# Score matmuls of the 90-row chunks over 40 columns, loads tied to the mixing, and one group's first layer on row halves of the array

## The chip, the core and the metric

One core of a Trainium2 chip runs the kernel. TensorE shows in the profile as PE (matmuls) and PEld (weight loads), VectorE as DVE, ScalarE as ACT, GpSimd as POOL, SyncE as SP; SP, POOL and, at the start, ACT also issue DMA transfers. The metric is the device time of one execution in microseconds (us), median of several runs.

## The reference

Talking-heads attention, then a two-layer network with a leaky activation. Shapes: batch 4, 12 heads, 448 tokens, head width 64; the network goes 768 -> 2048 -> 768.

```python
scores = scale * np.matmul(q, k.transpose(0, 1, 3, 2))
scores = np.einsum('bhij,hg->bgij', scores, w_pre)
scores = scores - np.max(scores, axis=-1, keepdims=True)
attn = np.exp(scores)
attn = attn / (np.sum(attn, axis=-1, keepdims=True) + 1e-09)
attn = np.einsum('bhij,hg->bgij', attn, w_post)
attn_out = np.matmul(attn, v)          # -> x, 1792 x 768
h = x @ w_in
g = np.maximum(h, 0.0) + alpha * np.minimum(h, 0.0)
out = g @ w_out
```

## The kernel before

**First phase (attention).** The 448 query rows of a batch are cut into four chunks of 120, 120, 120 and 90 rows (the last overlaps its neighbour by two). That gives 16 chunks, `ci` 0 to 15; chunks 3, 7, 11 and 15 have 90 rows. The steps, with the letter that the planner uses:

- **Q** (`qk`, L286): a score unit, one pair of heads of one chunk, six units in a chunk. It is four matmuls: two head halves (rows 0 to 63 and 64 to 127 of the array) by two column blocks of the chunk's query rows. The second block is what is left after 64: 56 columns for a 120-row chunk and 26 for a 90-row chunk. Each such float32 matmul stands in the trace as two instructions, so a unit is x8.
- **S** (`qk_out`, L299): ACT or DVE copies a unit's scores to SBUF.
- **L** (`relay`, L306): a DMA carries ten query rows of all heads into the layout that the mixing needs (tiles `sr`, eight buffers), issued by SP and POOL in turn.
- **M** (`mix`, L313): two relayed groups times the pre-mixing weights. There are 90. **R** (L318, DVE) takes the row maximum, **E** (L325, ACT) the exponentials, **N** (L331 to L335, DVE) the normalised post-mixing weights, **P** (`post`, L347, PE) the post-mixing, and **A** (L359, ACT or DVE) copies its result out.
- **V** (`pv`, L369): attention times values, two for each chunk; **XH**, **XL** (L383, L385) round the result into a high and a low part and **W** (L391) stores them.
- Loads: **LQ** (L263) the queries of a chunk, **LK** (L254) a pair of key tiles, **LV** (L270, L271) the values of a batch, **F** (L397) a 768 KB block of 64-bit weights, which **C** (L57 to L63, seven DVE operations) turns into float32. All four are issued on POOL's queue, where relays stand too.

Every engine works through its instructions in program order. The function `plan` writes that order once, at build time: a list scheduler with a cost for each step, a priority, predecessors and buffer counts. `at` is the earliest planned time of a step. A predecessor in the plan only orders the steps; an instruction itself waits for data and buffers alone.

**Second phase (network).** `FGROUPS` cuts the 16 blocks of hidden units into five groups; a unit `u` is one block `f` for one batch `bl`, 64 units in all, in the order group, batch, block. A unit's first layer `l1` (L541) is 18 matmuls of 128 rows x 128 columns over 448 tokens into one PSUM tile `h` (the pool has two buffers), then `act_op`: j=0 a scaled Relu on ACT (L554), j=1 on DVE (L556), j=2 and j=3 split the result into `g` (L558, L560). The second layer `l2` (L579) is 18 matmuls into six accumulators. PE's order is l1(u), l2(u-1), l1(u+1), l2(u), and so on. Group 4 (blocks 12 to 15) takes the batches in the order 0, 1, 2, 3, so units 52 to 55 are its batch 1.

Of the kernel before, what the change touches and what calls it, by code (L numbers as in the profile page):

```python
# [8 lines left out]
F32 = mybir.dt.float32  # L9
# [5 lines left out]
ALU = mybir.AluOpType  # L15
# [4 lines left out]
B, H, S, D = 4, 12, 448, 64  # L20
# [9 lines left out]
NCC = DM // 128  # L30
NFC = DFF // 128
NP = H // 2
# [3 lines left out]
RAHEAD = 3  # L36
# [2 lines left out]
FGROUPS = [[0, 1, 2], [3, 4, 5], [6, 7, 8], [9, 10, 11], [12, 13, 14, 15]]  # L39
NPRE = 3  # L40
NXS = 3
COST = {"Q": 0.82, "M": 0.82, "P": 1.0, "V": 2.15, "U": 3.7, "mode": 0.15, "R": 1.09, "E": 1.37, "N": 0.68}
HOP, DRAIN = 0.07, 0.2
LOOK = 0.3
# [21 lines left out]
def plan(groups, first, chunk_list):  # L66
# [5 lines left out]
    def op(name, engs, prio, preds=(), acq=(), rel=(), at=0.0):  # L72
        if isinstance(engs, tuple):
            engs = [engs]
        ops[name] = (engs, prio, list(dict.fromkeys(preds)), acq, rel, at)

    pe = lambda kind, mode="q": ("PE", COST[kind], DRAIN, mode)
    act = lambda d: ("ACT", d, HOP, "")
    dve = lambda d: ("DVE", d, HOP, "")
    dma = lambda d, l=3.0: ("DMA", d, l, "")  # L80

    for ci, (b, c) in enumerate(chunk_list):
        op(("LQ", ci), dma(1.0) if ci >= 2 else dma(0.0, 0.0), first[max(ci - 1, 0)] / 2 - RAHEAD - 5, acq=(("q", ci),))
        for p in range(NP):
            n = ci * NP + p
            prio = (n - NP) * 0.92 - 1
            op(("Q", ci, p), pe("Q"), prio, [("LQ", ci), ("LK", b, p // 2)], (("slot", (ci, p)),) + ((("st", ci),) if p == 0 else ()),
               ((("q", ci),) if p == NP - 1 else ()) + ((("k", b, p // 2),) if c == len(CHUNKS) - 1 and p % 2 else ()),
               at=5.5 + 1.1 * p if ci == 0 else 10.0)
            op(("S", ci, p), [act(0.92), dve(1.09)], prio, [("Q", ci, p)], rel=(("slot", (ci, p)),))  # L90
    for b in range(B):
        f4 = first[4 * b]
        for kk in range(NP // 2):
            op(("LK", b, kk), dma(1.2) if b else dma(0.0, 0.0), f4 / 2 - RAHEAD - 11 + kk, acq=(("k", b, kk),))
        op(("LV", b), dma(3.0), f4 / 2 + (4 if b else 0), acq=(("v", b),), at=18.0)
    for n, (ci, r) in enumerate(groups):
        op(("L", n), dma(0.8, 4.0), n / 2 - 1 - RAHEAD, [("S", ci, p) for p in range(NP)], (("sr", n),),
           (("st", ci),) if n + 1 == first[ci + 1] else ())
# [1 line left out]
    for m in range(NB):  # L100
# [5 lines left out]
        for g in range(2):  # L106
            ci = groups[2 * m + g][0]
            op(("A", m, g), [act(0.52), dve(0.63)], m + 1.7, [("P", m)],
               (("at", ci),) if 2 * m + g == first[ci] else (), (("pa", m),))
    for ci, (b, c) in enumerate(chunk_list):  # L110
        lb = (first[ci + 1] - 1) // 2
        mine = [("A",) + divmod(n, 2) for n in range(first[ci], first[ci + 1])]
        for hx in range(2):
            pr = lb + 3.3 + 1.5 * hx
# [5 lines left out]
    nh = 2 * NPRE  # L120
    for i in range(nh):
        pr = 6 + 11 * i
        op(("F", i), dma(2.0, 4.0), pr - 6, acq=(("cr", i),), at=20.0)
        for j in range(7):
            op(("C", i, j), dve((0.57, 0.57, 0.57, 0.96, 0.57, 0.96, 0.96)[j]), pr + 1.3 * j,
               [("C", i, j - 1) if j else ("F", i)] + ([("C", i - 1, 6)] if i and not j else []),
               (("ct", i),) if j == 1 else (), (("cr", i),) if j == 5 else ())
        op(("WS", i), dma(1.0), pr + 10, [("C", i, 6)], rel=(("ct", i),))
# [3 lines left out]
    for f in range(NPRE):  # L132
        op(("LW", f), dma(2.0, 6.0), NB - 9 + f, [("WS", i) for i in range(nh)], (("cr", ("w", f)),))
        for x in range(2):
            pr = NB - 3 + 1.2 * f + 0.6 * x
# [3 lines left out]
    for u in range(2):  # L139
# [6 lines left out]

    cap = {"slot": 3, "st": NXS, "sr": 2 * (RAHEAD + 1), "e": LAG + 1, "r": LAG + 1, "pa": 1, "at": 2, "q": 3, "k": 4, "v": 1,
           "xe": 2, "cr": 2, "ct": 2}
# [14 lines left out]
    while ready:  # L163
        best = None
        for n in ready:
            engs, prio, preds, acq, rel, at = ops[n]
# [3 lines left out]
            for e, d, l, md in engs:  # L170
                d += COST["mode"] if e == "PE" and md != mode else 0.0
                t = max(t0, idle[e])
# [26 lines left out]
def talking_heads_prelu(ctx: ExitStack, tc: tile.TileContext, q, k, v, w_pre, w_post, mask, w_in, w_out, alpha, out):  # L199
    nc = tc.nc  # L200
# [5 lines left out]
    groups, first = [], []  # L206
# [29 lines left out]
    ps = pool("ps", 1, p1, space=PSUM)  # L236
# [10 lines left out]
    k_t, q_t, v_t, s_t, a_t = {}, {}, {}, {}, {}  # L247
# [9 lines left out]
    def load_q(ci, dmas=None):  # L257
        b, c = chunk_list[ci]
        c0, cn = CHUNKS[c]
        q_t[ci] = qp.tile([128, NP * CW], F32, tag="q", name=f"q{ci}")  # L260
        for hf in range(2):
            dma = dmas[hf] if dmas else nc.gpsimd
            dma.dma_start(out=q_t[ci][64 * hf:64 * hf + 64, :NP * cn],  # L263
                          in_=q[b, :, QOFF[c] + NP * hf * cn:QOFF[c] + NP * (hf + 1) * cn])
# [10 lines left out]
    def slot_tile(i, name):  # L275
        return ps.tile([128, 2, 512], F32, tag=f"b{i}", name=name)

    def qk(ci, p, slot):
        b, c = chunk_list[ci]
        cn = CHUNKS[c][1]  # L280
        ps = slot_tile(slot, f"s{ci}_{p}")
        for hf in range(2):
            for ch in range(2):
                r = slice(64 * hf, 64 * hf + 64)
                i0, i1 = 64 * ch, min(64 * ch + 64, cn)
                nc.tensor.matmul(ps[i0:i1, hf, :S], q_t[ci][r, p * cn + i0:p * cn + i1], k_t[b, p // 2][r, p % 2, :],  # L286
                                 start=True, stop=True)
        u_t["qk", ci, p] = ps
# [132 lines left out]
    with tc.manual_schedule():  # L421
        start = p1r.enter_context(tc.tile_pool(name="start", bufs=1, side="right"))
# [24 lines left out]
        for i, w in enumerate((w_pre, w_post)):  # L447
# [15 lines left out]
            op=ALU.mult,  # L463
        )
        P2 = {}
# [8 lines left out]
        x_t, wi_t, wo_t, g_t, h_t, accs = {}, {}, {}, {}, {}, {}  # L474
# [59 lines left out]
        def l1(u, slot=None):  # L534
            gi, bl, f = units[u]
            w, x = wi_t[f], x_t[bl].bitcast(F32R)
            ps = P2["h"].tile([128, 512], F32, tag="h", name=f"h{u}") if slot is None else slot_tile(slot, f"h{u}")[:, 0]
            i = 0
            for cc in range(NCC):
                for tw, tx in ((0, 0), (0, 1), (1, 0)):  # L540
                    nc.tensor.matmul(ps[:, :S], w[:, tw, cc * 128:(cc + 1) * 128], x[:, tx, cc, :],  # L541
                                     start=(i == 0), stop=(i == 3 * NCC - 1))
                    i += 1
            h_t[u] = ps

        def act_op(u, j):
            f = units[u][2]
            h = h_t[u][:, :S]
            if j == 0:
                g_t[u] = (P2["gp"].tile([128, S], F32, tag="t", name=f"t{u}"),  # L550
                          P2["gp"].tile([128, 2, S], F32R, tag="g", name=f"g{u}"))
            t, g = g_t[u]
            if j == 0:
                nc.scalar.activation(out=t, in_=h, func=AF.Relu, scale=-1.0)  # L554
            elif j == 1:
                nc.vector.scalar_tensor_tensor(out=t, in0=t, scalar=oma[:, f:f + 1], in1=h, op0=ALU.mult, op1=ALU.add)  # L556
            elif j == 2:
                nc.scalar.copy(g[:, 0], t)  # L558
            else:
                nc.vector.tensor_tensor(g[:, 1], t, g[:, 0], ALU.subtract)  # L560
# [105 lines left out]
        def prefetch(u):  # L666
            nxt = []
            for _, bl, _ in units[u:]:
                if bl not in nxt:
                    nxt.append(bl)  # L670
                if len(nxt) == NXS:
                    break
            for bl in nxt[1:]:
                if bl not in x_in.values():
                    free = [i for i in range(NXS) if x_in.get(i) not in nxt]
                    load_x(bl, free[0])
# [54 lines left out]
```

## Time and profile before

| | us |
|---|---|
| median of 3 runs | 931.24 (928.26 to 932.08) |
| profiled execution, device time | 935.73 |
| its span, first to last instruction | 934.0 |
| PE busy in the span | 878.8 (94%) |
| DVE busy | 578.4 (62%) |
| ACT busy | 343.5 (37%) |

Busy shares are means over two phases that differ. The prediction therefore reads stretches: how busy each engine is between two moments, what PE waited for just before a matmul, and how far apart the starts of two neighbouring groups on PE lie. The printed duration of a matmul reaches past the start of the next one, since matmuls are pipelined; the distance of starts is what a group costs.

### The profile page before, as it was taken

The page shows a single profiled execution, that of the slowest core. Times are in us where ns is not written, and L with a number is a line of the kernel's source. Part 1 is how long each engine was busy: PE and PEld are TensorE (multiplying, and loading weights), DVE is VectorE, ACT ScalarE, POOL GpSimd, SP SyncE. Part 2 cuts the span into 40 slices and gives each one's busy share as a digit, 9 for nine tenths or more (in the row PEclk, how much of TensorE's full clock was granted, in tenths as well). Part 3 has the DMA queues.
Part 4 walks back from the last instruction along what each step waited for, and adds up shares of the span by engine and source line. Part 5 has one row for each costly group of instructions (what it writes and reads, how often), then busy time and mean ns, then how long its engine had stood idle before and what let it go on. Part 6 is the DMA issues. An engine that isn't in the chain of part 4 may idle for free.

```text
span 934.0 us, 23852 instructions
## 1 busy us (share of the span) xinstructions
PE 878.8 (94%) x10380; PEld 665.5 (71%) x10380; DVE 578.4 (62%) x1023; ACT 343.5 (37%) x718; POOL 110.6 (12%) x194
## 2 busy tenths in 40 slices
PE   8589998999889997998899999999999999979998
PEld 3354565456553665456899999999999999869997
DVE  4475787569854886456455566667666763873332
ACT  3453765357643675346222222121212211211110
POOL 5122223222311222000000000000000000000000
PEclk9799999999999999999999999999999999989999
DMA  7666677566754469754831242025012511232111
GB/s 194 188 191 154 185 220 205 157 197 181 217 156 129 137 204 251 225 175 131 259 151 34 68 151 70 34 68 185 35 34 68 186 34 35 68 106 106 60 60 59
DMA packets 70974, 125.36 MB, mean 134 GB/s; under 512 B 32614, under 2 KB 59246, under 8 KB 70870
## 3 DMA queue, kind: packets, MB, share of 16 engines
q0 software_dynamic: 15344, 59.22, 21.8%
q1 hardware_dynamic: 54866, 63.33, 21.4%
q8 instruction: 81, 1.33, 0.6%
q10 hardware_dynamic: 660, 1.30, 0.5%
q14 instruction: 23, 0.19, 0.1%
HBM read 66.16 MB, written 18.92 MB: 91 GB/s over the span
## 4 chain that ended last, share of the span: by engine, by line
PE 82%; DVE 6%; DMA 6%; ACT 3%; issue 2%; SPq 0%; POOL 0%; ACTq 0%; DVEq 0%; POOLq 0%
PE h L541 25%; PE acc L579 24%; PE s L286 13%; PE x L369 8%; PE pa L347 7%; PE m L313 7%; DMA sr<-st 5%; DVE at L359 1%; DVE nm L318 1%; ACT e L325 1%; DVE ao L591 1%; ACT st L299 1%; ACT at L359 1%; DMA k<-in_k_dram 1%; DVE ct L60 0%
## 5 line engine op out<-in xcount | busy, mean ns | idle before, releaser
L541 PE MATMUL h<-x,w 128*128 128x448 f32 x1152 | 250.5, 370 | 6.4 <-ACT w L504 6.3
L579 PE MATMUL acc<-g,w 128*128 128x448 f32 x1152 | 245.6, 366 | 2.0 <-DVE t L556 1.4
L541 PEld LDWEIGHTS h<-x,w 128*128 128x128 f32 x1152 | 217.3, 189 | 28.8 <-ACT w L504 6.7
L579 PEld LDWEIGHTS acc<-g,w 128*128 128x128 f32 x1152 | 216.1, 188 | 21.7 <-DVE t L556 1.7
L286 PE MATMUL s<-k,q 64*64 64x448 f32 (+2 forms) x768 | 159.9, 555 | 1.9 <-ACT st L299 0.6
L347 PEld LDWEIGHTS pa<-r,e 64*64 64x64 f32 x5040 | 100.0, 136 | 58.7 <-issue 33.2
L556 DVE SCALAR_TENSOR_TENSOR t<-t,oma,h 128x448 f32<-128x448 f32 x64 | 43.5, 680 | 157.8 <-ACT t L554 157.8
L554 ACT ACTIVATE t<-h 128x448 f32<-128x448 f32 x64 | 34.9, 545 | 268.1 <-PE h L541 268.1
L325 ACT ACTIVATE e<-m,nm 128x448 f32<-128x448 f32 x180 | 112.7, 636 | 31.6 <-DVE nm L318 20.4
L318 DVE TENSOR_REDUCE nm<-m 128x2 f32<-128x896 f32 x90 | 97.6, 1085 | 36.1 <-PE m L313 35.7
L347 PE MATMUL pa<-r,e 64*64 64x60 f32 x5040 | 105.8, 223 | 14.6 <-issue 9.4
L313 PE MATMUL m<-sr,wk 64*64 64x448 f32 x720 | 97.7, 566 | 21.6 <-DMA sr<-st 18.4
L286 PEld LDWEIGHTS s<-k,q 64*64 64x64 f32 (+2 forms) x768 | 37.2, 128 | 78.2 <-issue 65.0
L369 PEld LDWEIGHTS x<-at,v 128*64 128x64 f32 x1536 | 75.6, 138 | 20.1 <-issue 6.6
L359 DVE COPY at<-pa 128x480 f32<-128x480 f32 x83 | 53.8, 656 | 54.8 <-ACT at L359 30.4
L306 POOL DMA_DIRECT2D sr<-st x89 | 53.2, 600 | 286.2 <-PE m L313 189.6
L369 PE MATMUL x<-at,v 128*64 128x120 f32 (+1 forms) x1536 | 82.5, 264 | 3.7 <-DVE at L359 1.4
L299 ACT COPY st<-s 120x896 f32<-120x896 f32 (+1 forms) x65 | 58.6, 906 | 67.7 <-PE s L286 61.2
L359 ACT COPY at<-pa 128x480 f32<-128x480 f32 x97 | 53.8, 570 | 69.7 <-PE pa L347 55.1
L313 PEld LDWEIGHTS m<-sr,wk 64*64 64x64 f32 (+1 forms) x720 | 24.9, 134 | 55.1 <-DMA sr<-st 22.2
L558 ACT CAST g<-t 128x448 fp32r<-128x448 f32 x64 | 36.3, 567 | 53.9 <-DVE t L556 53.9
L591 DVE TENSOR_TENSOR ao<-ao,acc 128x448 f32<-128x448 f32 x96 | 52.7, 613 | 1.7 <-PE acc L579 1.7
(49 smaller groups left out, 522.3 us busy)
## 6 DMA issues: line engine op xcount, KB each, us to landing
x<-x SPq DMA_DIRECT2D x16, 1344.0 KB
sr<-st SPq DMA_DIRECT2D x89, 210.0 KB
sr<-st POOLq DMA_DIRECT2D x89, 210.0 KB, 4.8
cr<-in_w_in_dram POOLq DMA_DIRECT2D x16, 768.0 KB, 4.7
cr<-in_w_out_dram POOLq DMA_DIRECT2D x16, 768.0 KB, 4.6
x<-xe SPq DMA_DIRECT2D x48, 180.0 KB
out_dram<-ao SPq DMA_DIRECT2D x24, 224.0 KB
v<-in_v_dram POOLq DMA_DIRECT2D x4, 1152.0 KB, 9.3
```

The costliest lines, as they stand in the source:

```text
L286: nc.tensor.matmul(ps[i0:i1, hf, :S], q_t[ci][r, p * cn + i0:p * cn + i1], k_t[b, p // 2][r, p % 2, :], start=True, stop=True)
L299: copy(dst[:cn, p], u_t.pop(("qk", ci, p))[:cn, :, :S])
L306: dma.dma_start(out=sr_t[n][SR0:SR0 + GP], in_=s_t[ci][r:CHUNKS[chunk_list[ci][1]][1]:CHUNKS[chunk_list[ci][1]][1] // GI])
L313: nc.tensor.matmul(ps[hf:hf + 64, u, :S], wk[r, :], g[r, :], start=True, stop=True)
L318: nc.vector.tensor_reduce(out=nm, in_=m_t[m][:, :, :S], axis=AX.X, op=ALU.max, negate=True)
L325: nc.scalar.activation(out=e_t[m][:, u], in_=m_t[m][:, u, :S], func=AF.Exp, bias=nm_t[m][:, u:u + 1], scale=1.0, accum_out=se_t[m][:, u:u ...
L347: nc.tensor.matmul(dst[:, :, HI * u:HI * u + HI], e[h, u, 64 * jb:64 * jb + 64], r[h, u].rearrange("p (h i) -> p h i", h=H), start=True, s ...
L359: copy_on[eng](dst, pa[:, g, :NS * GP].rearrange("p (s i) -> p s i", i=GI))
L369: nc.tensor.matmul(ps[64 * t:64 * t + 64, 0, cl * CW:cl * CW + cn], v_t[b][:, s, h * D:(h + 1) * D], a_t[ci][:, s, h, :cn], start=(s == 0) ...
L541: nc.tensor.matmul(ps[:, :S], w[:, tw, cc * 128:(cc + 1) * 128], x[:, tx, cc, :], start=(i == 0), stop=(i == 3 * NCC - 1))
L579: nc.tensor.matmul(accs[c][:, :S], w[:, tw, c * 128:(c + 1) * 128], g[:, tg], start=(f == fs[0] and i == 0), stop=(f == fs[-1] and i == 2))
L591: nc.vector.tensor_tensor(acc_sb[c, bl], acc_sb[c, bl], accs[c][:, :S], ALU.add)
```

## The change

Three edits. (1) In `qk` the second column block of a 90-row chunk is 40 columns wide instead of 26; the extra columns read the next head's queries, or, for the last head, 14 zeroed columns that a POOL memset writes. Their output rows are not read. (2) In `plan`, the loads LQ, LK, LV and F get a mixing step M as predecessor, in place of a planned time for LV and F. (3) The first layer of units 52 to 55 runs as pairs of matmuls on rows 0 to 63 and 64 to 127 into two PSUM tiles, which ACT (a copy) and DVE (an addition) then bring together.

```diff
+MIN_M = 40
+ROWS = (4, 1)
...
-        op(("LQ", ci), dma(1.0) if ci >= 2 else dma(0.0, 0.0), first[max(ci - 1, 0)] / 2 - RAHEAD - 5, acq=(("q", ci),))
+        op(("LQ", ci), dma(1.0) if ci >= 2 else dma(0.0, 0.0), first[max(ci - 1, 0)] / 2 - RAHEAD - 5,
+           [("M", first[ci - 1] // 2 - RAHEAD - 7)] if ci > 3 else [("M", ci - 2)] if ci >= 2 else [], acq=(("q", ci),))
...
-            op(("LK", b, kk), dma(1.2) if b else dma(0.0, 0.0), f4 / 2 - RAHEAD - 11 + kk, acq=(("k", b, kk),))
-        op(("LV", b), dma(3.0), f4 / 2 + (4 if b else 0), acq=(("v", b),), at=18.0)
+            op(("LK", b, kk), dma(1.2) if b else dma(0.0, 0.0), f4 / 2 - RAHEAD - 11 + kk,
+               [("M", f4 // 2 - RAHEAD - 12 + kk)] if b else [], acq=(("k", b, kk),))
+        op(("LV", b), dma(3.0), f4 / 2 + (4 if b else 0), [("M", f4 // 2 + 2)], acq=(("v", b),))
...
-        op(("F", i), dma(2.0, 4.0), pr - 6, acq=(("cr", i),), at=20.0)
+        op(("F", i), dma(2.0, 4.0), pr - 6, [("M", pr - 3)], acq=(("cr", i),))
...
+        pad = 64 + MIN_M - cn
+        if pad > 0:
+            nc.gpsimd.memset(q_t[ci][:, NP * cn:NP * cn + pad], 0.0)
...
-                i0, i1 = 64 * ch, min(64 * ch + 64, cn)
+                i0, i1 = 64 * ch, 64 * ch + 64 if not ch else max(cn, 64 + MIN_M)
...
+            if (gi, bl) == ROWS:
+                ps2 = P2["h"].tile([128, 512], F32, tag="h", name=f"h{u}_2")
+                h_t[u, 2] = ps2
...
-                    nc.tensor.matmul(ps[:, :S], w[:, tw, cc * 128:(cc + 1) * 128], x[:, tx, cc, :],
-                                     start=(i == 0), stop=(i == 3 * NCC - 1))
+                    st = dict(start=(i == 0), stop=(i == 3 * NCC - 1))
+                    if (gi, bl) == ROWS:
+                        for r, o in ((0, ps), (64, ps2)):
+                            nc.tensor.matmul(o[:, :S], w[r:r + 64, tw, cc * 128:(cc + 1) * 128], x[r:r + 64, tx, cc, :], **st)
+                    else:
+                        nc.tensor.matmul(ps[:, :S], w[:, tw, cc * 128:(cc + 1) * 128], x[:, tx, cc, :], **st)
...
+            if (u, 2) in h_t:
+                if j == 0:
+                    hs_t[0] = P2["gp"].tile([128, S], F32, tag="hs", bufs=1, name=f"hs{u}")
+                hs = hs_t[0]
+                if j == 0:
+                    nc.scalar.copy(t, h_t[u, 2][:, :S])
+                    nc.vector.tensor_tensor(hs, t, h, ALU.add)
+                h = hs
```

On PE, a score unit of a 90-row chunk (chunk 3, first unit, and the P and M behind the second) stood so before:

```order
L286 MATMUL s_0_848<-k_0_122,q_463 64x448
L286 MATMUL s_0_848<-k_0_122,q_463 26x448
L286 MATMUL s_0_848<-k_0_122,q_463 64x448
L286 MATMUL s_0_848<-k_0_122,q_463 26x448
L286 MATMUL s_1_857<-k_0_122,q_463 64x448
```

and stands so now:

```order
L293 MATMUL s_0_848<-k_0_122,q_504 64x448
L293 MATMUL s_0_848<-k_0_122,q_504 40x448
L293 MATMUL s_0_848<-k_0_122,q_504 64x448
L293 MATMUL s_0_848<-k_0_122,q_504 40x448
L293 MATMUL s_1_858<-k_0_122,q_504 64x448
```

The place is the same and the number of matmuls too; only the width of every second one differs.

On POOL's queue, right after the constants have been loaded (q, k, v are loads, `cr` is F's block, `sr` are relays), the order before was:

```order
L263 DMA q_177<-in_q_dram 64x720 x2
L254 DMA k_0_180<-in_k_dram 64x896 x2
L306 DMA sr_111<-st_188 120x1x448
L306 DMA sr_108<-st_188 120x1x448
L306 DMA sr_106<-st_188 120x1x448
L269 MEMSET v_277 64x768
L270 DMA v_277<-in_v_dram 128x3x768
L271 DMA v_277<-in_v_dram 64x768
L397 DMA cr_0_308<-in_w_in_dram 128x768
L306 DMA sr_108<-st_188 120x1x448
```

and is now:

```order
L313 DMA sr_111<-st_182 120x1x448
L313 DMA sr_108<-st_182 120x1x448
L313 DMA sr_106<-st_182 120x1x448
L270 DMA q_264<-in_q_dram 64x720 x2
L313 DMA sr_112<-st_182 120x1x448
L313 DMA sr_109<-st_182 120x1x448
L276 MEMSET v_299 64x768
L277 DMA v_299<-in_v_dram 128x3x768
L278 DMA v_299<-in_v_dram 64x768
L404 DMA cr_0_357<-in_w_in_dram 128x768
```

The queries of chunk 2 moved behind three relays, the first key load of batch 1 left this stretch, and the values and the first weight block moved behind two more relays, whose buffers the first two mixings set free.

On ACT, the first two units of the batch on row halves (units 52 and 53) stood before as the Relu and the cast of each unit:

```order
L554 ACTIVATE t_9069<-h_9032 128x448
L558 CAST g_9070<-t_9069 128x448
L554 ACTIVATE t_9115<-h_9075 128x448
L558 CAST g_9116<-t_9115 128x448
L554 ACTIVATE t_9176<-h_9133 128x448
L558 CAST g_9177<-t_9176 128x448
```

and now, from the same unit 51 on, as:

```order
L578 ACTIVATE t_9073<-h_9036 128x448
L582 CAST g_9074<-t_9073 128x448
L574 COPY t_9138<-h_2_9080 128x448
L578 ACTIVATE t_9138<-hs_9140 128x448
L582 CAST g_9139<-t_9138 128x448
L574 COPY t_9221<-h_2_9160 128x448
L578 ACTIVATE t_9221<-hs_9223 128x448
L582 CAST g_9222<-t_9221 128x448
```

Each of the four units got a copy of its second PSUM tile ahead of the Relu, and the Relu now reads `hs`, the sum that one more DVE addition makes.

## Rows read from the trace of the kernel before

**Rows 1.** The page: engines' busy time in the span; shares of the last-ending chain.

```profile
PE 878.8 (94%) x10380; PEld 665.5 (71%) x10380; DVE 578.4 (62%) x1023; ACT 343.5 (37%) x718; POOL 110.6 (12%) x194
...
PE 82%; DVE 6%; DMA 6%; ACT 3%; issue 2%; SPq 0%; POOL 0%; ACTq 0%; DVEq 0%; POOLq 0%
```

**Rows 2.** Stretches: length, busy us PE PEld DVE ACT POOL, clock, DMA share, GB/s.

```profile
66.63:97.12 30.49, 30.49 (x359) 11.16 (x355) 15.41 (x31) 11.73 (x26) 5.84 (x11) 1.00 0.62 167
97.12:166.43 69.31, 64.96 (x1585) 41.96 (x1585) 54.30 (x105) 47.09 (x108) 18.70 (x32) 0.98 0.71 205
166.43:196.78 30.35, 30.35 (x359) 11.09 (x355) 15.75 (x34) 11.86 (x26) 6.14 (x11) 1.00 0.58 167
196.78:272.29 75.51, 67.72 (x1633) 45.47 (x1633) 57.10 (x113) 48.42 (x109) 18.56 (x31) 0.98 0.67 187
272.29:302.68 30.39, 30.39 (x357) 11.12 (x353) 15.28 (x27) 11.31 (x26) 5.24 (x10) 1.00 0.51 144
302.68:372.15 69.47, 62.77 (x1585) 42.98 (x1585) 55.26 (x107) 46.07 (x106) 15.36 (x26) 0.98 0.67 194
372.15:405.42 33.27, 33.27 (x412) 13.70 (x404) 14.33 (x28) 11.31 (x26) 2.30 (x4) 1.00 0.57 180
```

**Rows 3.** Timeline of PE: start, length; a 90-row score unit, the mixing behind it.

```profile
75.33 3.53 PE L286 MATMUL s<-k,q 64*64 64x448 f32 x8
78.79 0.98 PE L313 MATMUL m<-sr,wk 64*64 64x448 f32 x8
```

**Rows 4.** The same view: a 120-row score unit, and what follows it.

```profile
106.50 0.98 PE L286 MATMUL s<-k,q 64*56 64x448 f32 x8
107.33 1.09 PE L347 MATMUL pa<-r,e 64*64 64x60 f32 x54
```

**Rows 5.** Score matmuls by shape (rows*columns), whole span: count, busy, mean ns.

```profile
L286 PE MATMUL s<-k,q 64*56 64x448 f32 x288 | 69.2, 558 | 0.0
...
L286 PE MATMUL s<-k,q 64*26 64x448 f32 x96 | 44.7, 545 | 0.0
```

**Rows 6.** Timeline of weight loads in the unit of rows 3.

```profile
76.17 0.12 PEld L286 LDWEIGHTS s<-k,q 64*26 64x26 f32 x2 [0.70 <-issue]
77.04 0.19 PEld L286 LDWEIGHTS s<-k,q 64*64 64x64 f32 x2 [0.74 <-issue]
```

**Rows 7.** Timeline of PE at the start: mixings and their waits.

```profile
25.12 0.98 PE L313 MATMUL m<-sr,wk 64*64 64x448 f32 x8 [1.37 <-DMA sr<-st]
32.87 1.01 PE L313 MATMUL m<-sr,wk 64*64 64x448 f32 x2 [6.76 <-DMA sr<-st]
```

**Rows 8.** Timeline of POOL at the start: issues of values and first weight block.

```profile
18.42 0.80 POOL L270 DMA_DIRECT2D v<-in_v_dram  x1
...
19.76 0.57 POOL L397 DMA_DIRECT2D cr<-in_w_in_dram  x1
```

**Rows 9.** DMA issues: count, size of each, median us from issue to landing.

```profile
cr<-in_w_in_dram POOLq DMA_DIRECT2D x16, 768.0 KB, 4.7
...
v<-in_v_dram POOLq DMA_DIRECT2D x4, 1152.0 KB, 9.3
...
q<-in_q_dram POOLq DMA_DIRECT2D x22, 180.0 KB, 5.6
```

**Rows 10.** Timeline, second phase: first layer of unit 52 and what follows.

```profile
837.66 3.70 PEld L541 LDWEIGHTS h<-x,w 128*128 128x128 f32 x18
837.86 3.88 PE L541 MATMUL h<-x,w 128*128 128x448 f32 x18
...
841.58 3.81 PE L579 MATMUL acc<-g,w 128*128 128x448 f32 x18
841.84 0.55 ACT L554 ACTIVATE t<-h 128x448 f32<-128x448 f32 x1 [4.71 <-PE h L541]
...
843.73 0.62 DVE L560 TENSOR_TENSOR g<-t,g 128x448 fp32r<-128x448 f32 x1 [0.63 <-ACT g L558]
...
845.23 3.88 PE L541 MATMUL h<-x,w 128*128 128x448 f32 x18
```

## What I expected before the run

> **What bounds the kernel now.** I read the page first: PE is busy for 94% of the span and carries 82% of the chain that ended last [rows 1]. So the question is what PE does in each stretch, not what it waits for on average. I then cut the first phase at the score units of the 90-row chunks, because the view by shape shows a third form there, 26 columns wide, with 44.7 us of busy time for only 96 instructions, where 288 instructions of 56 columns take 69.2 us [rows 5]. The stretches show two kinds [rows 2]. In the four short ones, each with the six score units of one 90-row chunk, PE is busy for all of the time while DVE has 14.3 to 15.8 us of work in 30.4 to 33.3 us and ACT about 11.5. In the three long ones between them PE has 94%, 90% and 90%, DVE 78%, 76% and 80%, ACT 68%, 64% and 66%. So PE is the bound everywhere, but in the short stretches it is alone, and everything else catches up there.
>
> **Why those units are dear.** A score unit of a 120-row chunk starts at 106.50 and the next group on PE at 107.33: 0.83 us for eight instructions of some 555 ns, which can only be if four of them run side by side, on two row halves and two column blocks [rows 4, 5]. The unit of a 90-row chunk starts at 75.33 and the mixing behind it at 78.79: 3.46 us for as many instructions [rows 3]. Its weight loads show why: those of the 26-column block come at 76.17, those of the next 64-column block only at 77.04, 0.87 us later, after 0.74 us in which nothing that the profile shows held them back [rows 6]. So its four blocks run one after another, each as long as a whole ordinary unit.
>
> **Edit 1, 40 columns.** The number of instructions stays, so all that changes is whether the blocks run side by side. No row shows 40 columns. The rows on either side of it are 56 (side by side) and 26 (not). If 40 behaves like 56, a unit saves 3.46 - 0.83 = 2.63 us of PE, and 96 / 4 = 24 units (two row halves, two instructions each) save 63.1 us. If it behaves like 26, it saves nothing. I take the side of 56: that 56 and 64 run together shows that equal widths are not needed, and the loss at 26 is whole, so there is a step between the two and not a slope. Where it lies, the rows leave open, so the other side is a rival (below). The Trainium skill has a rule on this (TensorEngine Tiling (Array Packing), section Tiling Modes): column tiles come in widths of 128, 64 and 32, tiles of one mode work independently, and a change of the mode drains the array. By that rule 26 columns are a 32-wide tile beside 64-wide ones, and 40 columns are a 64-wide one; the trace agrees with its first half, 0.87 us a block, and the sum by it is the one that I make.
>
> The saving is PE's own time; what reaches the end is less. From 66.63 to 405.42, 338.8 us, PE is busy for 319.95 us (the seven PE values of rows 2 added). Without 63.1 it needs 256.8. If all the waiting there, 18.8 us, stayed as it is, the stretch would take 275.7 and all 63.1 us would be gained. That is the upper end. But the short stretches would then hold 14.6 us of PE work beside 15.4 of DVE, and stop being the place where the others catch up. At the other end I let them be set by DVE at its share in the long stretches, 166.7 of 214.3 us or 78%: their 60.8 us of DVE work take 78.1 us instead of 124.5, a gain of 46.4. In between, I let the whole run at the PE share of the long stretches as they are now. Their mean is 0.91; I take 0.90, that of two of the three, since they lose their head start: 256.8 / 0.90 = 285.4 us, a gain of **53.4 us**. DVE would then have 227.4 of 285.4 us, 80%, ACT 187.8 or 66%: what the long stretches bear today. That these would be as full there as anywhere is the reason to stay away from the upper end. The four POOL memsets are 14 columns each, on an engine busy for 12% [rows 1]: nothing.
>
> **Edit 2, the loads.** At the start, values (1152 KB) and the first weight block (768 KB) are issued at 18.42 and 19.76, just ahead of the relays that the second and third mixing need; PE waits for relays 1.37 and 6.76 us there [rows 7, 8]. In the new order two more relays, which wait for the first mixings, stand ahead of them. So up to 8.1 us can go. What is late next is the first conversion: its block now starts behind those relays and behind the values, which take 9.3 us to land, and DVE reaches its first conversion step after five mixings instead of eight; R, N and A stand behind it on DVE, and P and M on PE wait for those. If its whole landing of 4.7 us [rows 9] were exposed, 4.7 us would go back. I take a gain of **4.0 us**, half of the waits, with -4.7 and +8.1 as ends. Everywhere else the loads move by a few steps: counted in program order, queries stand six to nine mixings ahead of their first use (three for chunk 2), keys five to eight, weight blocks one to three where it was five to fifteen. Even if all 90 mixings lay within the 285 us above they would be 3.2 us apart, so that two make over 6 us, against 5.6 us for queries and 4.7 for a block [rows 9]. I cost that at nothing, hidden by PE's own work; if the cover fails it is DVE that stands at the conversion (a rival, below).
>
> **Edit 3, row halves.** The first layer takes 841.58 - 837.86 = 3.72 us, 0.207 for each of 18 matmuls [rows 10]. In four units 72 matmuls become 72 pairs. The nearest rows are the score units, where two row halves do run side by side [rows 4]; then a pair costs what one did, and there are only the changes of shape, into and out of the halves, eight in all. A block after a change of shape took 0.87 us where a whole unit took 0.83 [rows 4, 6]: 0.04 each, **+0.3 us**. If the halves follow one another, each as long as now, the cost is 4 x 3.72 = 14.9 us. A gain I bound by the rate of the second layer, 3.65 us for 18: 0.3 us. The added copy and addition (0.55 and 0.62 us by the like rows of ACT and DVE) lie beside the second layer: both PSUM tiles are free again by about 843.1, and the next first layer starts at 845.23; `g` is done 1.2 us later than at 844.35, and is needed at 845.23 + 3.72 = 848.95 [rows 10]. Without that cover it would be at most 1.2 us a unit.
>
> A rule of the Trainium skill speaks against this edit (TensorE: Matmul & The Clock Gate, Part 3, "What overlaps and what doesn't"): weight loads overlap with running matmuls only where the row groups differ. By it, each half would have to wait for its own load. The trace does not agree for whole rows: 18 loads of 128 rows take 3.70 us, within the 3.72 us in which the matmuls on the same 128 rows run [rows 10]. By the rule, 72 x 0.206 = 14.8 us would come on top, the same as the serial halves below.
>
> **Sum.** -53.4 - 4.0 + 0.3 = -57.1. The profiled execution took 935.73, so it would take 878.6. It lies 4.5 us above the median of the runs, 931.24; for the median I expect **874 us**.
>
> **Rivals.**
> *Serial halves.* The two halves of a first layer follow one another, by either mechanism above: 874 + 14.6 = 889. For it: no row shows 64 rows by 128 columns in this number format. Against it: the score units. Chance 0.17.
> *The others become the bound.* The short stretches are set by DVE, 46.4 us, and at the start a wait for the conversion takes the place of the relays: 931.2 - 46.4 + 0.3 = 885. For it: DVE's 15.4 us against PE's 14.6. Against it: ACT has 2 to 4 us less than DVE there, and the copies S and A are spread over both. Chance 0.17.
> *All of it.* The waits stay as they are and the start gains 8.1: 931.2 - 63.1 - 8.1 + 0.3 = 860. Chance 0.07.
> *The change doesn't do what it says.* 40 columns run like 26: 931.2 - 4.0 + 0.3 = 927.5, a change within the measurement. For it: no row shows 40 columns. Against it: the loss is a step, and 40 lies in the upper half of the 64. Chance 0.03.
> *Slower than before.* DVE stands at the first step of each of the six conversions until the block has landed, with R and N behind it. It must cost more than 57.1 + 4.7 = 61.8 us, 10.3 us a block, to be slower by 0.5%. With 4.7 us a block it would be 902; only if each landed as late as values and block together, 14 us, would it be 958. Against it: DMA engines are busy for 0.51 to 0.71 of the time. Chance 0.02.
>
> **How the numbers follow.** The forecast has the remaining 0.54. A change of under 0.5%, 4.7 us, cannot be told from none here. The range from 858 to 898 holds the forecast, the serial halves (889), the other engines as the bound (885) and the full gain (860), and leaves out the sum of the two bad cases (about 900) and the last two rivals. All cases but the last two are faster by far more than 0.5%: 0.95 faster, 0.03 the same, 0.02 slower.
>
> **What would show it.** Score units of 90-row chunks at about 0.83 us from start to start; the stretches from the first to the last of them near 285 us, with PE at about 0.90; the third mixing at the start before 30 us; first layers of units 52 to 55 of about 3.75 us. The prediction is wrong if the PE share in the first phase falls under 0.86 (256.8 / 0.86 = 299, 13 us more), if DVE shows idle time that a weight block ended, or if a half-row layer takes 7.4 us.

## The result and the profile after

| | us |
|---|---|
| before, median of 4 runs | 931.66 (928.26 to 939.15) |
| after, median of 4 runs | 889.54 (882.68 to 901.38) |
| ratio, 95% interval | 0.951 (0.939 to 0.963) |
| profiled execution, before and after | 935.73 and 883.63 |
| forecast for the median | 874 (858 to 898) |

The kernel is 4.9% faster. The ratio leaves out the slowest of the four runs after, whose mean granted clock was the lowest, 0.970. Between the profiled executions lie 52.1 us, where the sum forecast 57.1. Divided at the same events (M82 is the 83rd of the 90 mixings, with which the last short stretch ends), the spans of 934.0 and 881.8 us differ so:

| part of the span | before | after | difference | forecast |
|---|---|---|---|---|
| start to the first unit of chunk 3 | 66.63 | 67.44 | +0.8 | -4.0 |
| from there to M82, the seven stretches of [rows 2] | 338.8 | 284.5 | -54.3 | -53.4 |
| M82 to the first layer of unit 0 | 34.1 | 34.9 | +0.8 | 0 |
| second phase | 494.4 | 495.0 | +0.6 | +0.3 |

The view of busy time by stretch, cut at the same units as in [rows 2] (length, then busy us of PE, PEld, DVE, ACT and POOL, the granted clock, the DMA share, GB/s), shows the gain where it was looked for. The short stretches went from 30.5 to some 15.2 to 16.1 us and the last from 33.3 to 20.4; the long ones stayed at 69 to 78. PE is busy for 258.3 us in all, where 319.95 stood before and 256.8 was forecast. A share of 0.908 follows; 0.90 was forecast.

```profile
67.44:82.62 15.18, 14.55 (x357) 9.12 (x357) 13.70 (x31) 13.58 (x33) 5.26 (x10) 1.00 0.96 236
82.62:151.90 69.28, 64.61 (x1584) 41.81 (x1578) 56.07 (x107) 45.23 (x104) 18.54 (x33) 0.98 0.74 210
...
168.00:245.90 77.90, 68.11 (x1634) 44.99 (x1632) 58.59 (x121) 48.89 (x112) 18.40 (x33) 0.96 0.72 200
...
331.50:351.93 20.43, 17.53 (x419) 11.95 (x413) 13.10 (x25) 11.14 (x26) 1.95 (x4) 1.00 0.88 274
sum 284.49, PE 258.28 PEld 170.20 DVE 225.43 ACT 186.83 POOL 71.08; mean PE 36.90 PEld 24.31 DVE 32.20 ACT 26.69 POOL 10.15
```

PE's timeline shows a unit of a 90-row chunk from start to start: 70.62 to 71.45, 0.83 us, what the 120-row unit of [rows 4] takes, in place of the 3.46 us of [rows 3].

```profile
70.62 0.98 PE L293 MATMUL s<-k,q 64*40 64x448 f32 x8
71.45 1.09 PE L354 MATMUL pa<-r,e 64*64 64x60 f32 x54
```

Waiting in these stretches rose from 18.8 to 26.2 us. The view of PE's waits by releaser (us in total, times, longest) says of what kind, for the kernel before from 66.63 to 405.42:

```profile
PE pa L347 <- issue: 7.2, 4, 3.0
PE m L313 <- DMA sr<-st: 6.5, 5, 2.9
PE x L369 <- issue: 1.0, 1, 1.0
...
PE m L313 <- issue: 0.2, 1, 0.2
```

and for the kernel after from 67.44 to 351.93:

```profile
PE pa L354 <- issue: 11.7, 9, 2.5
PE m L320 <- DMA sr<-st: 6.8, 5, 2.9
PE x L376 <- issue: 1.8, 1, 1.8
...
PE m L320 <- issue: 0.9, 1, 0.9
```

Waits for relays stayed (6.5 and 6.8). Waits for nothing that the profile shows, "issue", went from 8.4 to 14.4 us, and these 6.0 are most of the 7.4. No wait of DVE for a weight block appeared.

At the start PE waits for relays for 7.5 us in all, where it waited 10.2 before (1.79, 0.27, 1.37 and 6.76). The second mixing gets its second relay later, at 27.97 in place of 25.12. The third gets its own sooner: its second half starts at 29.52, within the row of 27.97, in place of 32.87 [rows 7]. PE's timeline after:

```profile
20.25 0.98 PE L320 MATMUL m<-sr,wk 64*64 64x448 f32 x8 [1.76 <-DMA sr<-st]
21.89 0.97 PE L320 MATMUL m<-sr,wk 64*64 64x448 f32 x4 [0.65 <-DMA sr<-st]
...
27.97 3.25 PE L320 MATMUL m<-sr,wk 64*64 64x448 f32 x12 [5.11 <-DMA sr<-st]
...
55.70 0.50 PE L354 MATMUL pa<-r,e 64*64 64x60 f32 x19 [2.74 <-issue]
...
57.10 4.15 PE L376 MATMUL x<-at,v 128*64 128x120 f32 x48
61.17 0.98 PE L320 MATMUL m<-sr,wk 64*64 64x448 f32 x8
```

What is gained there is lost again by 67: 2.74 us of an "issue" wait, and behind it the 48 matmuls of V take 61.17 - 57.10 = 4.07 us, where before they took 2.61. PE's timeline before:

```profile
57.45 2.68 PE L369 MATMUL x<-at,v 128*64 128x120 f32 x48 [0.85 <-ACT e L325]
60.06 1.03 PE L347 MATMUL pa<-r,e 64*64 64x60 f32 x50
```

The granted clock there after the change, from the view by stretch, is the lower level, 1.2 GHz:

```profile
56.70:60.11 3.41, 3.41 (x34) 3.02 (x32) 2.81 (x7) 0.90 (x3) 1.25 (x2) 0.51 0.32 111
```

The row halves, in PE's timeline of the second phase:

```profile
784.72 3.91 PE L554 MATMUL h<-x,w 64*128 64x448 f32 x36
788.56 3.90 PE L603 MATMUL acc<-g,w 128*128 128x448 f32 x18
792.40 3.91 PE L554 MATMUL h<-x,w 64*128 64x448 f32 x36
```

36 half-row matmuls take 3.84 us, the second layer behind them 3.84 too: 7.68 a unit, where a whole unit took 845.23 - 837.86 = 7.37 [rows 10]. So +0.3 a unit, +1.2 for four.

### The profile page after: what moved, and what is told of

Its sections match the earlier page's. It is cut to its first block, busy times and chain, and to the rows that moved or that the text cites. A ratio compares the mean times of both kernels' runs of the same rounds, so it can differ in the third digit from the quotient of the medians.

```text
span 881.8 us, 23984 instructions
## 1 busy us (share of the span) xinstructions
PE 824.0 (93%) x10452; PEld 662.4 (75%) x10452; DVE 580.2 (66%) x1026; ACT 344.5 (39%) x723; POOL 110.1 (12%) x198
## 4 chain that ended last, share of the span: by engine, by line
PE 82%; DVE 7%; ACT 4%; DMA 4%; issue 3%; ACTq 0%; DVEq 0%
PE acc L603 25%; PE h L556 24%; PE x L376 9%; PE pa L354 8%; PE m L320 7%; PE s L293 6%; DMA sr<-st 4%; PE h L554 2%; DVE at L366 1%; ACT e L332 1%; DVE nm L325 1%; ACT at L366 1%; ACT st L306 1%; DVE ao L615 1%; DVE ce L64 1%
## 5 line engine op out<-in xcount | busy, mean ns | idle before, releaser
L556 PE MATMUL h<-x,w 128*128 128x448 f32 x1080 | 236.0, 372 | 6.4 <-ACT w L511 6.3
L556 PEld LDWEIGHTS h<-x,w 128*128 128x128 f32 x1080 | 204.7, 190 | 27.6 <-ACT w L511 6.7
L354 PEld LDWEIGHTS pa<-r,e 64*64 64x64 f32 x5040 | 102.0, 137 | 70.4 <-issue 36.3
L580 DVE SCALAR_TENSOR_TENSOR t<-t,oma,h 128x448 f32<-128x448 f32 x60 | 40.8, 680 | 137.3 <-ACT t L578 137.3
L354 PE MATMUL pa<-r,e 64*64 64x60 f32 x5040 | 108.5, 225 | 23.6 <-issue 15.9
L578 ACT ACTIVATE t<-h 128x448 f32<-128x448 f32 x60 | 32.6, 544 | 244.6 <-PE h L556 244.6
L320 PE MATMUL m<-sr,wk 64*64 64x448 f32 (+1 forms) x720 | 102.8, 584 | 17.6 <-DMA sr<-st 14.3
L325 DVE TENSOR_REDUCE nm<-m 128x2 f32<-128x896 f32 x90 | 97.6, 1085 | 26.3 <-PE m L320 25.9
L293 PE MATMUL s<-k,q 64*64 64x448 f32 (+2 forms) x768 | 99.9, 557 | 1.3 <-ACT e L332 0.5
L313 POOL DMA_DIRECT2D sr<-st x89 | 53.4, 603 | 255.5 <-PE m L320 165.7
L320 PEld LDWEIGHTS m<-sr,wk 64*64 64x64 f32 (+1 forms) x720 | 27.9, 138 | 48.3 <-issue 15.8
L584 DVE TENSOR_TENSOR g<-t,g 128x448 fp32r<-128x448 f32 x64 | 39.9, 623 | 14.7 <-ACT g L582 14.7
```

Source lines behind the costliest of these rows:

```text
L313: dma.dma_start(out=sr_t[n][SR0:SR0 + GP], in_=s_t[ci][r:CHUNKS[chunk_list[ci][1]][1]:CHUNKS[chunk_list[ci][1]][1] // GI])
L320: nc.tensor.matmul(ps[hf:hf + 64, u, :S], wk[r, :], g[r, :], start=True, stop=True)
L325: nc.vector.tensor_reduce(out=nm, in_=m_t[m][:, :, :S], axis=AX.X, op=ALU.max, negate=True)
L354: nc.tensor.matmul(dst[:, :, HI * u:HI * u + HI], e[h, u, 64 * jb:64 * jb + 64], r[h, u].rearrange("p (h i) -> p h i", h=H), start=True, s ...
```

## The experiments

"Before" is run again beside each. A ratio is to the kernel before, with its 95% interval.

**1. 40 columns alone.** Only the first edit, nothing of the loads or the row halves.

```diff
+MIN_M = 40
...
-                i0, i1 = 64 * ch, min(64 * ch + 64, cn)
+                i0, i1 = 64 * ch, 64 * ch + 64 if not ch else max(cn, 64 + MIN_M)
```

> Edit 1 alone: 40 columns, old load order, no row halves. Theory A (the score units give nearly the whole gain; loads and row halves together are worth under 3 us): the first layer of unit 0 starts within 4 us of 386.9, and the profiled time is 880 to 886. Rival B (the loads carry a part of 5 us or more of the gain): unit 0 starts after 392 and the time is 889 or more. Rival C (the loads cost time in the changed kernel): unit 0 starts before 382 and the time is under 878.

Measured: 885.55 us, ratio 0.949 (0.944 to 0.955), against 0.951 for the whole change. Unit 0 starts at 383.93 in the profiled execution of 881.29, so theory A holds: the whole gain is in this edit, and the other two together add nothing.

**2 and 3. 32 and 33 columns.** The same edit with another width.

```diff
-MIN_M = 40
+MIN_M = 32
```

> Edit 1 with 32 columns in place of 40, nothing else changed. Theory A (the dear form is that of a block that fits in 32 columns; a step just above 32): a score unit of a 90-row chunk stays at 3.46 us from start to start and the time stays at 928 to 939. Rival D (the step lies between 26 and 32, or the cost falls with the width): the units take under 3 us and the time is clearly under 925.

> Edit 1 with 33 columns, nothing else changed. Theory A (step just above 32): a unit takes 0.75 to 0.85 us and the time is that of 40 columns alone, 880 to 890. Rival D (step between 33 and 40, or a slope): the unit takes over 1.5 us, the time is over 895.

Measured: 929.65 us with 32, 878.94 with 33 (one run each; the latter 1 us under theory A's 880). The view by shape, first of 32, then of 33:

```profile
L290 PE MATMUL s<-k,q 64*64 64x448 f32 x384 | 113.1, 551 | 2.5 <-ACT st L303 0.7 <-DMA k<-in_k_dram 0.7 <-ACT e L329 0.5
...
L290 PE MATMUL s<-k,q 64*32 64x448 f32 x96 | 44.9, 548 | 0.0
```

```profile
L290 PE MATMUL s<-k,q 64*64 64x448 f32 x384 | 92.1, 554 | 2.2 <-ACT st L303 1.0 <-ACT e L329 0.5 <-DVE xe L389 0.4
...
L290 PE MATMUL s<-k,q 64*33 64x448 f32 x96 | 23.0, 562 | 0.0
```

32 columns behave like 26 [rows 5], 33 like 40: 44.9 us of busy time against 23.0, and the 64-column blocks beside them give back 21.0 more. So it is a step, between 32 and 33, and not the amount of work: one column more takes 51 us off. The Trainium skill (TensorEngine Tiling (Array Packing), Tiling Modes) has column tiles of 32, 64 and 128 and a drain at a change of mode. The trace agrees with the widths, since the step lies just above 32. That a drain is what keeps the blocks of such a unit from running side by side would fit its 3.46 us [rows 3]; no row shows the drain itself.

**4. The loads alone.** Only the second edit, at 26 columns.

```diff
-        op(("LV", b), dma(3.0), f4 / 2 + (4 if b else 0), acq=(("v", b),), at=18.0)
+        op(("LV", b), dma(3.0), f4 / 2 + (4 if b else 0), [("M", f4 // 2 + 2)], acq=(("v", b),))
```

and likewise LQ, LK and F.

> Edit 2 alone: the loads tied to the mixing, 26 columns, no row halves. Theory A: no difference that can be measured (0.995 to 1.005); PE's waits for relays at the start fall from 8.1 to about 5.8 us, but as in the changed kernel something else takes their place before 66 us. Rival B: 0.5% or more faster, with the score units of chunk 3 starting 4 us earlier than at 66.6.

Measured: 940.60 us, ratio 1.009 (1.005 to 1.012). Slower, where -4 us was forecast and neither theory had a loss.

**5 and 6. The loads in two halves.** LV and F tied alone; LQ and LK tied alone.

> The kernel before with the value loads and the first conversion tied to mixings, the query and first-matrix loads left as they were, 26 columns, no row halves. Theory A (what costs is that values and weight block now come late and together at the start and land beside the relays of the fourth and fifth mixing, where V runs at half clock): most of the loss of the loads as a whole, +0.5 to +0.9%. Rival B (the query and first-matrix loads, which now wait in a queue ahead of others): 0 to +0.2% here. Rival C, my forecast for the loads: -0.4%.

> The kernel before with the query loads and the loads of the first matrix tied to mixings, the value loads and conversions left as they were, 26 columns, no row halves. Theory A (values and weight block carry the loss): within 0.2% of before. Rival B (these loads carry it): +0.5 to +0.9%, with new waits of PE for score operands at the first unit of a chunk.

Measured: LV and F 938.81 us, 1.006 (1.002 to 1.009); LQ and LK 948.01 us, 1.018 (1.014 to 1.022). Both cost; theory A, by which the query loads would be free, is out, and so is any simple sum, since both together cost less than the queries alone.

The first mixings on PE's timeline, all loads tied, then LV and F, then LQ and LK, and last the kernel of experiment 7 below, whose first phase is that of before:

```profile
22.75 3.19 PE L315 MATMUL m<-sr,wk 64*64 64x448 f32 x12 [4.10 <-DMA sr<-st]
27.87 2.02 PE L315 MATMUL m<-sr,wk 64*64 64x448 f32 x12 [1.93 <-DMA sr<-st]
```

```profile
21.75 1.72 PE L313 MATMUL m<-sr,wk 64*64 64x448 f32 x12 [1.90 <-DMA sr<-st]
26.49 2.41 PE L313 MATMUL m<-sr,wk 64*64 64x448 f32 x12 [3.02 <-DMA sr<-st]
...
40.05 1.01 PE L313 MATMUL m<-sr,wk 64*64 64x448 f32 x2 [5.70 <-DMA sr<-st]
```

```profile
22.06 3.16 PE L315 MATMUL m<-sr,wk 64*64 64x448 f32 x12 [3.08 <-DMA sr<-st]
30.77 3.25 PE L315 MATMUL m<-sr,wk 64*64 64x448 f32 x12 [5.54 <-DMA sr<-st]
```

```profile
22.71 3.25 PE L313 MATMUL m<-sr,wk 64*64 64x448 f32 x12 [2.68 <-DMA sr<-st]
27.56 1.72 PE L313 MATMUL m<-sr,wk 64*64 64x448 f32 x12 [1.60 <-DMA sr<-st]
```

The last block shows that the wait of 6.76 us belongs to the one profiled execution of before, and not to its load order. Five profiles have the old order at the start. In four of them (40, 32 and 33 columns alone and experiment 7) the third mixing's second half starts at 27.7 to 29.4, and chunk 3 at 62.05 to 63.27; only in that of before are they at 32.87 and 66.63. Why it was late there is open.

With LV and F tied, there is a long wait at the sixth mixing, from 34.35 on, and chunk 3 starts at 66.62: values are issued at 25.06, the weight block at 26.41 and that mixing's second relay right behind them, at 27.50. With LQ and LK tied, the queries of chunk 2 no longer stand ahead of the first relays but behind them, at 17.38, just before values and weight block at 19.23 and 20.53; the wait is now the second mixing's, the mixings behind it come later, and chunk 3 starts at 72.94. With all of them tied the waits for relays before the second phase are 12.5 us, less than the 18.4 in the profile of before, but not than the 11.6 and 8.5 with 32 columns and in experiment 7. Chunk 3 starts at 65.62, and PE takes 390.5 us for the same instructions from 14 us on, where it took 385.7. The view by stretch, before and then all loads tied:

```profile
14.00:439.55 425.55, 385.67 (x7863) 220.85 (x7855) 283.06 (x554) 235.42 (x539) 88.04 (x149) 0.98 0.64 183
```

```profile
14.00:441.14 427.14, 390.49 (x7859) 222.55 (x7851) 283.13 (x553) 235.27 (x540) 89.90 (x153) 0.97 0.64 184
```

The granted clock is 0.97 in place of 0.98: 27.3 us at the lower level in place of 20.5 (23.9 with 32 columns, 13.7 in experiment 7). It was 34.1 us with either half of the loads tied. The first layer of unit 0 starts at 441.14, 1.6 us later than before, but 7.3 and 9.9 us later than with 32 columns (433.83) and in experiment 7 (431.29); the medians differ by 7.1.

**7. Row halves in all 16 units of the last weight group.** At 26 columns, loads as before; beside the third edit of the change:

```diff
-            if (gi, bl) == ROWS:
+            if gi == 4:
```

> The kernel before with row halves in all 16 units of the last weight group instead of four, nothing else changed. Theory A: the pairs of half rows run side by side at the price of one whole matmul, and only the change of shape into and out of the halves costs, some 0.3 us a unit as in the four units of the changed kernel: 16 x 0.3 = +4.8 us, and the starts of the two matmuls of a pair lie under 10 ns apart. Rival: the four units looked cheap for want of neighbours, and with halves throughout the second half of a pair waits for its weights: 16 x 3.7 = +59 us. Second rival: the extra copy and addition on ACT and DVE of every unit make PE wait before each second layer, which adds over 1 us a unit, +16 us or more.

Measured: 935.79 us in one run, beside 931.27 of before. PE's timeline:

```profile
857.00 3.97 PE L547 MATMUL h<-x,w 64*128 64x448 f32 x36
860.90 3.92 PE L596 MATMUL acc<-g,w 128*128 128x448 f32 x18
864.75 3.97 PE L547 MATMUL h<-x,w 64*128 64x448 f32 x36
```

A unit takes 864.75 - 857.00 = 7.75 us, 0.38 over a whole one, 6 us for 16. Theory A holds; halves one after another would have taken 11 us a unit, and no wait for ACT or DVE stands in these rows. In the changed kernel the two starts of a pair are 2 to 5 ns apart and pairs follow at 203 ns, below the 207 of whole matmuls; the first pair takes 305 ns and the first step of the second layer 307. The cost is the two changes of shape, some 0.1 us each and a gap.

**8. Half of PE's instructions in the post-mixing.** The changed kernel with one matmul of 120 columns for two of 60; the exponentials of the second half are left out.

```diff
-        for u in range(2):
-            for jb in range(NJ):
...
-                    nc.tensor.matmul(dst[:, :, HI * u:HI * u + HI], e[h, u, 64 * jb:64 * jb + 64],
-                                     r[h, u].rearrange("p (h i) -> p h i", h=H), start=True, stop=True)
+        for jb in range(NJ):
...
+                nc.tensor.matmul(dst, e[h, 0, 64 * jb:64 * jb + 64],
+                                 r[h].rearrange("p u (h i) -> p h u i", h=H), start=True, stop=True)
```

> The changed kernel with half of PE's instructions in the post-mixing: both row halves of weights are multiplied with the first half's exponentials, in one matmul of 120 columns instead of two of 60, so the exponentials of the second half are left out. 16 instructions fewer for every mixing, the same columns. Theory A (the new waits of PE that nothing in the profile holds back are waits for its own instructions, which the stretches of the first phase now use up faster): these waits before the second phase fall from 18.6 us to under 8 us, and the time falls by 10 to 20 us, partly because short matmuls go too. Rival B (they come from the clock or from the order of the work): they stay between 14 and 22 us, and what is gained is PE's own time alone.

Measured: 870.16 us in one run. PE's waits before the second phase, from 14 us on, after and then in this kernel:

```profile
PE pa L354 <- issue: 15.9, 11, 2.7
PE m L320 <- DMA sr<-st: 14.3, 8, 5.1
...
PE x L376 <- issue: 1.8, 1, 1.8
```

```profile
PE m L320 <- DMA sr<-st: 26.3, 15, 5.6
PE pa L353 <- DVE at L365: 4.7, 6, 1.4
```

The "issue" waits are gone, from 18.6 us (with 0.9 at L320) to none, and not only in the post-mixing, and the time is 13.5 us under that of the profiled execution after, as theory A had it. But 12.0 us came back as waits for relays (14.3 to 26.3). The view by stretch from 14 us to the second phase, after and then in this kernel:

```profile
14.00:386.86 372.86, 328.49 (x7858) 217.01 (x7850) 281.73 (x553) 234.00 (x540) 89.72 (x157) 0.96 0.75 211
```

```profile
14.00:373.85 359.85, 318.76 (x5366) 204.38 (x5358) 280.33 (x553) 234.04 (x540) 89.97 (x157) 0.97 0.77 218
```

Of the 13.0 us that this stretch loses, 9.7 are PE's own time and 3.3 waiting (44.4 to 41.1): what the "issue" waits cost the end is nearer 3 than 18.6. That the gain is mostly PE's own time is what rival B had said. The DMA queue of instructions, on the pages after and of this kernel (packets, MB, share), says the same:

```profile
q8 instruction: 82, 1.34, 0.6%
```

```profile
q8 instruction: 62, 1.02, 0.5%
```

5,040 instructions fewer and 0.32 MB less: 64 bytes each, in packets of 16 KB. One stall at close range, on PE's timeline after, with a single packet of this queue between 225.0 and 228.5 (the DMA share there is mostly 0.8 or more):

```profile
225.60 0.29 PE L354 MATMUL pa<-r,e 64*64 64x60 f32 x5
228.35 1.04 PE L354 MATMUL pa<-r,e 64*64 64x60 f32 x51 [2.46 <-issue]
```

Where the stalls come settles what they are. Count PE's instructions in the trace, weight loads and those of its queue with them. The first behind each of the thirteen "issue" waits after is then number 194 or 195 beyond a multiple of 256 (1,218, 2,499, 9,155 and so on), and the same holds for all eight of before. 256 instructions of 64 bytes are one packet, and each of the thirteen waits ends 1.3 to 1.7 us after such a packet has landed. So these waits are PE's waits for its next block of instructions; an instruction waits for more than its data and buffers.

The Trainium skill (Runtime: NRT & Kernel Launch, Terms) says that an engine's instruction memory is refilled in blocks of 16 KiB; the packets agree.

**9. Values loaded once.** The changed kernel without three value loads.

```diff
     def load_v(b):
+        if b:
+            v_t[b] = v_t[0]
+            return
```

> The changed kernel without the value loads of the last three batches, whose outputs then use the first batch's values: three loads of 1152 KB fewer, every wait and every other load left. Theory A (the waits of PE for relays at 140, 229 to 240 us come from relays that share the DMA engines with a value load): PE's waits for relays before the second phase fall from 14.3 us to 9 us or less, and what is left is that of the start, some 7.5 us. Rival B (the relays are late because the store behind them is, and the loads are not to blame): they stay within 2 us of 14.3. The waits for PE's own instructions, 18.6 us, should stay over 14 us by both, if no DMA traffic of the loads is behind them; if they fall with the loads, the instruction fetch is slowed by them.

Measured: 871.26 us in one run. Waits for relays 10.3 us, "issue" 12.0. The waits for relays at 140 and 229 to 240 are gone, but others came, 3.1 us at 255.7 and 1.6 at 342, so neither theory's number is met: the loads bear on the waits, and are not their only cause. The "issue" waits are a third shorter with no instruction less on PE, and under the 14 us that were to hold if the loads had no part in them. That the fetch is slower beside the loads fits, but is not shown by this one run: in other profiles with as many instructions in the first phase these waits are 14.3 us (33 columns), 14.6 (40 columns alone) and 19.8 (experiment 11).

**10 and 11. A candidate, and the two first edits together.** 40 columns with each batch's values loaded in four pieces, other loads as before; and 40 columns with all loads tied.

```diff
-        op(("LV", b), dma(3.0), f4 / 2 + (4 if b else 0), acq=(("v", b),), at=18.0)
+        for s in range(NS):
+            op(("LV", b, s), dma(0.9), f4 / 2 + 4 + s if b else f4 / 2 + s, [("M", f4 // 2 + 5 + s if b else s + 2)],
+               acq=(("v", b),) if s == 0 else (), at=18.0)
...
```

> A candidate: 40 columns, query and first-matrix loads and conversions as before the change, no row halves, and each batch's values loaded in four pieces, tied to four mixings in turn. Theory A (a value load of 1152 KB in one piece holds up the relays behind it): waits for relays fall from 14.1 us (40 columns alone) to about 9 us, and the time lies 3 to 6 us under that of 40 columns alone, ratio to before 0.943 to 0.947. Rival B (the sum of the bytes counts, or the tie of a load to a mixing costs by itself, as with the loads alone): 0 to 8 us over 40 columns alone, ratio 0.949 to 0.958.

> 40 columns and all loads tied to the mixings, no row halves: the changed kernel without its third part. Theory A (the tied loads cost in the new kernel about what they cost in the old one, +0.6 to +1.2%): 5 to 10 us over 40 columns alone, ratio to before 0.954 to 0.960. Rival B (with the short stretches the ties help, or cost nothing): ratio 0.945 to 0.951. The row halves are worth +1.2 us by the profile, so this one should lie within 2 us of the changed kernel by both.

Measured: the candidate 882.53 us, 0.947 (0.942 to 0.951); all loads tied 891.91 us, 0.955 (0.950 to 0.960). The candidate's waits for relays are not shorter (14.3 us), so theory A's mechanism fails, though its ratio came out, and the lead of 3 us on 40 columns alone is within the intervals. That the tied loads cost in the new kernel too is likely (891.91 against 885.55 and 882.53), and the intervals still overlap. The view by stretch, 40 columns alone, then with all loads tied:

```profile
14.00:383.93 369.93, 328.51 (x7861) 216.22 (x7853) 282.01 (x554) 234.76 (x539) 87.84 (x153) 0.97 0.74 211
```

```profile
14.00:400.74 386.74, 334.74 (x7859) 217.44 (x7851) 281.69 (x553) 234.61 (x540) 89.75 (x157) 0.94 0.72 203
```

The latter is the longest of its six runs, 896.18: PE waits 10.6 us longer (52.0 against 41.4) and is busy 6.2 us longer for the same work, at a mean granted clock of 0.94.

## Why the prediction was right, point by point

**Edit 1** was right in place and mechanism: the unit takes 0.83 us, and 54.3 us went off the stretches for 53.4 forecast. It chose 56 as the neighbour of 40 over 26; the runs with 32 and 33 show why that was right. That the size came out so closely is partly luck. The same seven stretches took 331.3 us in experiment 7, whose first phase is that of before, not 338.8, and 298.5 in the longest run of experiment 11, not 284.5; between the medians of experiment 1 lie 48.0. That the waits would grow was right, but not the reason: the other engines, DVE above all, were to be as full as in the long stretches. DVE is (79%), but what grew was PE's wait for its own instructions, by 6.0 of 7.4 us, which the forecast's list of waits did not hold. Experiment 8 shows what they are, and also that without them relays would have held PE instead.

**Edit 2** failed, at the step from the waits of 1.37 and 6.76 us to "So up to 8.1 us can go". It took the waits of one execution for a property of the load order. In the four other profiles with that order the third mixing is as early as with the loads tied (27.7 to 29.4, against 29.52), so there was little to gain; the wait at the conversion that was feared did not come either. Against the profile of before the start changed by +0.8 in place of -4.0. Against the kernels with 40 and 33 columns alone chunk 3 starts some 5 us later after the change (67.44 against 62.66 and 62.05), with a longer "issue" wait and V at the lower clock. And the bytes were still to be moved: tied to a mixing, they can stand before the relays of a later one, as with LV and F. Alone the edit costs 0.5% to 1.2%. Why the query loads tied alone cost twice what all ties cost together is open; against experiment 7 their profile shows 10.0 us at the start.

**Edit 3** was right in kind, side by side, and small; the term of +0.3 us was mis-sized. It is +1.2: a change of shape costs some 0.1 us and a gap here, not the 0.04 of the score units. Waiting for a load on the same rows, 14.8 us by the Trainium skill's rule weighed there (TensorE: Matmul & The Clock Gate, Part 3, "What overlaps and what doesn't"), does not show; the measurement decides.

**The sum** was 5.0 us off the profiled execution (878.6 and 883.63), 4.8 of them the start. The other 10.5 us to the median are runs: the profiled one is 5.9 us under its median, where that of before was 4.5 above the median that the forecast had. The late start of that execution may have been counted twice, once as 4.0 us to gain and once in these 4.5. Rivals: "all of it" is excluded by the waits (26.2 us for 18.8), serial halves by the timeline, 40 columns that run like 26 by the unit. "The others become the bound" gave a nearer time, 885, by a mechanism that was not there: PE's waits for DVE in the stretches are 2.5 us in all, where they were 1.6 before.

## What to carry to other kernels

When a matmul takes part of the array, look at which widths share a form: 64 and 33 columns ran side by side, 64 and 32 did not, and padding by 14 columns halved the short stretches. After such a gain, ask what PE now uses up faster, its instructions among it, and count how many bytes of program an operation is. Before a wait is put into a sum, see whether a second profile of the same order has it. A load moved away from one wait is still to be moved: follow it to the next transfer that needs the same engines, and time the move by itself.

## What was not expected of the hardware

- PE waited for instructions, up to 2.7 us at a time (3.7 in experiment 11) and 18.6 us in all, while the DMA engines were busy for 0.75 of the time, each time at the border of a block of 256 instructions; with 5,040 instructions fewer there was no such wait.
- Each of the lower-clock pieces before the second phase in the changed kernel (26.0, 56.7, 142.1, 230.8, 323.0 and 367.3) begins in a wait of PE or up to 1.1 us behind one; these waits took 5.11, 2.74, 1.63, 2.93, 2.45 and 1.41 us. Others as long as some of these, as those at 83.37 and 209.08 (1.61 and 1.82 us), were followed by none.
- Pairs of half-row matmuls in this number format ran at 203 ns a pair, whole ones at 207.
